# VectorE's order at joined pairs: the sum of the odd products, the next block's attention work and the masked copies change places in its queue

## The chip, the cores and the metric

The kernel runs on one core of one Trainium2 chip. A core has five engines that work side by side, each through its own queue of instructions in a fixed order: TensorE multiplies matrices (PE in the profile, and PEld for its weight loads), VectorE (DVE) works elementwise, ScalarE (ACT) computes functions and copies, GpSimd (POOL) and SyncE (SP) do little here but small fills and the issue of DMAs. Engines meet only at semaphores: an instruction whose input is not ready waits, and all that stands behind it in the same queue waits with it. TensorE writes its results to PSUM, a small memory from which VectorE and ScalarE fetch them. The metric is the device time of one execution in microseconds (us), lower is better. A profiled execution also leaves a trace, with the start and the duration of each instruction.

## The reference

Two parts, all in fp32. The first is a linear attention with a decaying state, for 4 batches, 8 heads, 768 tokens and a head size of 48; the second is a two-layer network over the 3072 tokens of width 384, with an inner width of 2048:

```python
for t in range(S):
    kt, vt, rt, wt = (k[:, :, t], v[:, :, t], r[:, :, t], w[:, :, t])
    cur = np.einsum('bhd,bhe->bhde', u[None] * kt, vt)
    y[:, :, t] = np.einsum('bhd,bhde->bhe', rt, state + cur)
    state = wt[:, :, :, None] * state + np.einsum('bhd,bhe->bhde', kt, vt)
...
x = np.ascontiguousarray(attn_out.transpose(0, 2, 1, 3)).reshape(B * S, H * D)
h = x @ w_in
g = h - np.tanh(h)
return (g @ w_out).astype(np.float32)
```

## The kernel before

**Blocks and tiles.** The tokens are cut into 8 blocks of 384 (half a batch each). The main loop (L1348) goes over the blocks `i`; within a block the loop over `f` (L1358) goes over the 16 tiles of 128 columns of the inner width. While the network of block `i` runs, the attention of block `i + 1` (`later`) is computed in pieces that stand between the tiles' work, and its first steps are taken one block earlier still (`after`). Which piece comes at which `f` is written in `plan` (L1142): `before` and `ahead` list VectorE's pieces, `phases` TensorE's and ScalarE's, `loads` the DMAs that are issued.

**One tile.** `first` (L893) multiplies the block by the tile's weights into the PSUM tile `hp`. `slight` (L974) has ScalarE compute two hyperbolic tangents of it and one square with a maximum check (L984, L985, L988), and leaves VectorE one product, `g` (L902), which is put into the list `rest` and runs in the next `f`.

**Second layer.** Two tiles make a pair `q = f // 2`. Instead of 18 products of 128 by 128 a pair takes 15, of sums of pieces of `g`: `form_g` (L1003, recorded at L1007) makes two such sums in one VectorE instruction. After an even tile there is one form (n = 0), after an odd tile one (n = 2), which the list `formed` holds; three more (n = 4, 6, 8) are held back to the next pair's time in `forming` and `carried`. `Fewer.add` (L1090) issues 12 of the 15 products into the PSUM tiles `acc`, in two halves, two and three steps after the odd tile (the list `due`, `add_due`). The remaining three, the odd products, go through `Fewer.others` (L1102) into a PSUM buffer `apart`: pairs 0 to 3 at `f` = 9, pairs 4 to 6 and pair 7 at `f` = 0 and 1 of the next block. `others_summed` (L1114, one VectorE instruction at L1115) then adds both halves out of `apart`.

**Joined pairs.** For some pairs both tiles' first layer is computed together with 11 products instead of 12: `Twos.begin` (L945, TensorE at L958, 22 recorded matmuls of 128 by 192). It writes both of the two PSUM buffers named `att`, and VectorE makes the two tiles of `h` of them by four sums `outs` (L968), with a copy by ScalarE (L959). `JOINED` (L123) says which: pairs 1, 3, 4 and 7 in blocks 3 to 6, so `f` = 2 and 3, 6 and 7, 8 and 9, 14 and 15; pairs 4 and 7 in block 2; pairs 0 to 6 in block 7, which has no `later`. The even `f` of a joined pair issues the products and the four sums, the odd `f` the tangents of the second tile.

**Who else uses the two `att` buffers.** The odd products (`apart`), the scores of the attention (`earlier`, L520, TensorE at L504) at `f` = 4 in blocks 3 to 6, which VectorE copies under a mask into the tile `scores` by two instructions (`masked`, L512), and the state update and the results (L585, L781) at `f` = 10 and 12.

**VectorE's queue.** It is written out by hand, at L1407 to L1444: for each `f` a list `ops` is put together out of

- `rest`: `g` of the tile before,
- `formed`, `forming`, `carried`: forms of `g`,
- `outs`: the four sums of a joined pair,
- `behind`: what a TensorE phase or `others` left for VectorE, the masked copies and `others_summed`,
- `spare`: pieces of attention work and, at some `f`, sums of the block before (`sum`, L1118, at L1123).

`between` interleaves two lists. The pieces of attention work that the change touches are `times_behind` (L449, at L453), `times_before` (L443, at L446; it finishes `pre`, which the scores at `f` = 4 read), `product_u` (L390, at L392; it reads the tile `k` that the DMA of L388 fills with tokens), `held` (L473), `product_r` (L394, at L396), `product_sum` (L398, at L400), and `before` (L423: a reciprocal and a scan at L427).

Of the kernel before, what the change touches and what calls it, by code (L numbers as in the profile page):

```python
# [122 lines left out]
JOINED = {2: (4, 7), 3: BESIDE, 4: BESIDE, 5: BESIDE, 6: BESIDE, 7: TWOS}  # L123
# [12 lines left out]
def kernel(  # L136
# [1005 lines left out]
    def plan(i):  # L1142


        formed_w = {}
        if i == 0:
            phases = {6: ("turn",), 7: ("update",), 10: ("earlier",), 13: ("results",)}
            before = {0: ("behind 2", "take_whole 2"), 2: ("behind 0", "take_whole 0"), 3: ("times_behind 2",),
                      4: ("times_behind 0",), 5: ("before 2",), 6: ("before 0",), 7: ("times_before",),
                      9: ("product_u", "held", "bound 2"), 10: ("product_r", "bound 0"), 11: ("product_sum",), 12: ("diagonal_in 2", "diagonal_in 0")}  # L1150
            ahead = {}
            loads = {f: "weights" for f in (0, 1, 3, 4, 5, 6, 7, 8, 9, 10)}
            loads.update({2: "next r", 11: "w", 13: "k", 14: "r"})
            loads = {f: [name] for f, name in loads.items()}
            loads[3] += ["v", "row"]
            loads[4] += ["tokens k"]
            loads[9] += ["tokens r"]
        else:
            phases = {3: ("split 2 0",), 4: ("earlier", "split 2 1", "turned 2", "split 0 01"), 5: ("turned 0",),
                      6: ("join 2 0",), 7: ("join 2 1",), 8: ("join 2 2",), 9: ("join 0 02",), 10: ("update",),  # L1160
                      12: ("results",)}
            before = {0: ("times_behind 2",), 1: ("times_behind 0",), 3: ("times_before", "held"),
                      5: ("product_u",), 6: ("product_r",), 7: ("product_sum",), 8: ("diagonal_in 2",),
                      9: ("diagonal_in 0",)}
            ahead = {10: ("bound 2", "bound 0"), 11: ("behind 2", "take_whole 2"), 12: ("behind 0", "take_whole 0"),
                     13: ("before 2",), 15: ("before 0",)}
            loads = {1: ["v"], 3: ["tokens k"], 4: ["tokens r"], 7: ["w"], 9: ["k"], 11: ["r"]}
            if i in JOINED:
                before = {0: ("times_behind 2",), 1: ("times_behind 0", "times_before 2"),
                          2: ("times_before 0",), 3: ("held",), 4: ("product_u",), 7: ("product_r",), 9: ("product_sum",),  # L1170
                          10: ("diagonal_in 2", "diagonal_in 0")}
                phases.update({3: (), 4: ("earlier", "turned 2")})
                loads = {2: ["tokens k"], 4: ["tokens r"], 5: ["v"], 7: ["w"], 9: ["k"], 11: ["r"]}
        if i == 1:
            phases = {4: ("split 2 0",), 5: ("split 2 1", "turned 2"), 6: ("split 0 01",),
                      7: ("earlier", "turned 0", "join 2 0"), 8: ("join 2 1",), 9: ("join 2 2", "join 0 01"),
                      10: ("join 0 2",), 11: ("update",), 13: ("results",)}
            before = {0: ("behind 2", "take_whole 2", "bound 2"), 1: ("behind 0", "take_whole 0"),
                      2: ("times_behind 2",), 3: ("before 2", "bound 0"), 4: ("times_behind 0",), 5: ("before 0",),
                      6: ("times_before", "held"), 7: ("product_u",),  # L1180
                      9: ("product_r", "product_sum", "diagonal_in 2"), 10: ("diagonal_in 0",)}
            ahead = {12: ("bound 2",), 13: ("behind 2", "take_whole 2"), 14: ("bound 0",)}
            loads = {1: ["v"], 4: ["tokens k"], 6: ["tokens r"], 9: ["w"], 11: ["k"], 12: ["r"]}
            formed_w = {2: (0, 1), 7: (2, 3, 4, 5), 9: (6,), 10: (7, 8), 11: (9,), 12: (0, 1), 13: (2, 3, 4, 5, 6),
                        14: (7, 8, 9)}
        elif i == 2:
            phases.update({3: (), 4: ("split 2 0",), 5: ("earlier", "split 2 1", "turned 2", "split 0 01"),
                           6: ("turned 0", "join 2 0")})
            before = {0: ("behind 0", "take_whole 0", "times_behind 2"), 1: ("times_behind 0",), 2: ("before 2",),
                      3: ("before 0",), 4: ("times_before", "held"), 5: ("product_u",), 7: ("product_r",),  # L1190
                      9: ("product_sum",), 10: ("diagonal_in 2", "diagonal_in 0")}
            loads = {1: ["v"], 3: ["tokens k"], 5: ["tokens r"], 8: ["w"], 10: ["k"], 11: ["r"]}
        return phases, before, ahead, loads, formed_w
# [17 lines left out]
    def converting(pieces, n):  # L1211

        made = []
        for _ in range(n):
            if not pieces:
                on_act, on_dve = convert(*raws.pop(0))
                pieces += zip(on_act, ([], [], on_dve))
            op, then = pieces.pop(0)
            op()
            made += then  # L1220
        return made
# [102 lines left out]
    def between(ops, others):  # L1324

        n = min(len(ops), len(others))
        return [op for pair in zip(ops, others) for op in pair] + ops[n:] + others[n:]
# [20 lines left out]
    for i, blk in enumerate(blocks):  # L1348
# [9 lines left out]
        for f in range(NF):  # L1358
# [9 lines left out]
            elif f % 2 == 0:  # L1368
                for op in behind:
                    op()  # L1370
                behind = []
# [3 lines left out]
                        later.phase(ps_a, name)  # L1375
            if not i:
                made_up = converting(pieces, PIECES[f] if f < len(PIECES) else 0)
            if joined and f == 9:
                fewer.others(ps_a, range(4), hp)
            if joined and f % 2:  # L1380
# [25 lines left out]
            if not now:  # L1406
                ops = square + converting(pieces, 2)  # L1407
            elif now == 1:
                ops = rest + late + square + converting(pieces, 3)
            elif not i:  # L1410
                ops = extra + square + (rest + behind + spare if f < 7 else rest[:1] + behind + spare + rest[1:])
            elif outs and near:
                ops = between(rest, carried) + spare + outs[:1] + formed + outs[1:]
                carried = []
            elif outs and later:
                ops = between(rest, carried) + outs[:1] + formed + outs[1:] + spare
                carried = []
            elif outs:
                ops = (between(rest, carried) + outs[:1] + formed + spare[:-1] + outs[1:2] + spare[-1:] + outs[2:])
                carried = []  # L1420
            elif joined and later:
                ops, carried = forming[:1] + rest + formed + spare, forming[1:]
            elif joined and f < 2 * LAST:
                ops, carried = forming[:1] + between(rest + formed, spare), forming[1:]
            elif joined:
                ops = forming[:1] + between(rest, forming[1:])
            elif carried:
                ops, carried = between(rest + formed, carried + behind + spare), []
            elif forming:
                ops = between(rest, forming[:2]) + square + formed + forming[2:]  # L1430
                ops = (between(ops, behind) if len(behind) > 2 else ops + behind) + spare
            elif adding and f % 2:
                ops = adding[:2] + between(rest, adding[2:3]) + square
                adding = adding[3:]
            elif adding:
                at = n_whole + n_excess
                ops = (between(rest, behind) +
                       [lambda: nc.vector.tensor_single_scalar(holds[:, n_whole:at], excess, 0.0, op=ALU.is_le),
                        lambda: sum_held(holds[:, at:at + n_top - 2], top[:, 0:n_top - 2], holds[:, 0:at + n_top - 2],
                                         ends[:, 0:1])] + adding[:4] + square + adding[4:])  # L1440
            elif square:
                ops = (between(rest, behind) if len(behind) > 2 else rest + behind) + square + formed + extra + spare
            else:
                ops = between(rest + formed, behind + spare)  # L1444
# [50 lines left out]
            for name in loads.get(f, ()):  # L1495
# [8 lines left out]
                    ins = of.load_v() if name == "v" else of.load(name.split()[-1])  # L1504
                if ins:
                    begin_behind(made, ins)
            if f < 2 and summed:
                summed[0].others(ps_a, ((4, 5, 6), (7,))[f], None if later else hp)
                if f:
                    behind.append(summed[0].others_summed)  # L1510
            add_due(now)
# [94 lines left out]
```

## Time and profile before

| | us |
|---|---|
| median of 3 runs | 545.23 (544.53 to 546.56) |
| profiled execution, its own time | 545.7 |
| its span, first to last instruction | 543.9 |
| TensorE matmuls busy | 529.9 |
| TensorE weight loads busy | 438.2 |
| VectorE busy | 462.7 |
| ScalarE busy | 309.7 |

The profile of one execution is read in several views. The page gives busy time, the granted clock of TensorE and the chain of work that ended last, followed back from the last instruction. The view of the waits adds up who waited for whom: the total, the number of times and the longest. The timeline lists instructions in the order of time: start in us, duration in us, engine, line, operation, written tile `<-` read tiles, shape, and how many like ones in a row (`x8`); in brackets stands the idle time of the engine ahead of it and what ended it. A matmul in fp32 is recorded twice, so the 11 products of a joined pair are 22 records. Matmuls are pipelined: the next one starts before the one ahead has ended, and how far apart two of them start tells more than the end that the record gives.

### The profile page before, as it was taken

Reading aid. Unit: us, or ns where it says so; the run is one execution under the profiler, and the core shown is the slowest. Engines: PE = TensorE matmul, PEld = TensorE weight load, DVE = VectorE, ACT = ScalarE, POOL = GpSimd, SP = SyncE. Lnnn points to the kernel's source line nnn. Section 1 sums busy time; section 2 is a strip of 40 time slices with the busy share of each in tenths; the row PEclk is TensorE's granted clock in tenths of the full one; section 3 lists DMA queues with packets and bytes.
Section 4 is the critical chain, followed back from the end, with each engine's and each line's share of the span. In section 5 each row is a group of like instructions: output and inputs, shape, how many; then the busy total and the mean of one; then the engine's idle time right before and its main releaser. Section 6 shows DMA issues by size and latency. Waiting matters only on the chain.

```text
span 543.9 us, 14925 instructions
## 1 busy us (share of the span) xinstructions
PE 529.9 (97%) x5950; PEld 438.2 (81%) x5950; DVE 462.7 (85%) x970; ACT 309.7 (57%) x720; POOL 9.1 (2%) x57
## 2 busy tenths in 40 slices
PE   7999999999999999999999999999999999999996
PEld 5756665678787978989898888889888897899994
DVE  7889996799899798978997899977999779777874
ACT  5899984665536564547546374364735545435460
POOL 1100000000000000000000000000000000000001
PEclk9899999999999999999999999999999999999999
DMA  7798642343312532270313712146231510100011
GB/s 276 245 390 332 239 120 70 123 111 89 99 46 61 147 117 57 63 167 20 119 56 74 176 60 68 47 109 141 64 96 34 135 39 1 57 1 2 11 34 46
DMA packets 53046, 56.33 MB, mean 104 GB/s; under 512 B 21488, under 2 KB 50928, under 8 KB 52976
## 3 DMA queue, kind: packets, MB, share of 16 engines
q1 hardware_dynamic: 52592, 55.18, 34.2%
q8 instruction: 49, 0.80, 0.6%
q14 instruction: 21, 0.17, 0.1%
q10 hardware_dynamic: 288, 0.10, 0.1%
q0 software_dynamic: 96, 0.07, 0.1%
HBM read 44.73 MB, written 4.72 MB: 91 GB/s over the span
## 4 chain that ended last, share of the span: by engine, by line
PE 76%; DVE 19%; issue 2%; DMA 1%; ACT 1%; SPq 0%; DVEq 0%
PE hp L895 20%; PE acc L1088 20%; PE att L958 14%; PE acc L1039 6%; DVE g L1007 4%; PE hp L1088 3%; DVE pre L427 2%; PE att L504 2%; DVE post L439 2%; PE att L781 2%; DVE g L902 2%; PE att L1088 2%; PE att L585 2%; DVE states L597 1%; PE acc L1066 1%
## 5 line engine op out<-in xcount | busy, mean ns | idle before, releaser
L895 PE MATMUL hp<-xT,w_sb 128*128 128x384 f32 x438 | 154.2, 488 | 0.0
L1088 PE MATMUL acc<-forms,g 128*128 128x128 f32 x972 | 136.4, 276 | 0.0
L1088 PEld LDWEIGHTS acc<-forms,g 128*128 128x128 f32 x972 | 124.2, 192 | 4.6 <-DVE g L1007 0.3
L895 PEld LDWEIGHTS hp<-xT,w_sb 128*128 128x128 f32 x438 | 78.6, 190 | 44.1 <-issue 1.4
L1007 DVE TENSOR_TENSOR g<-g 128x256 f32<-128x256 f32 x270 | 107.4, 421 | 4.6 <-PE acc L1088 0.3
L902 DVE SCALAR_TENSOR_TENSOR g<-h,qa 128x384 f32<-128x384 f32 x112 | 61.9, 552 | 37.5 <-ACT h L988 37.0
L984 ACT ACTIVATE h<-hp 128x384 f32<-128x384 f32 x73 | 36.3, 497 | 94.0 <-PE hp L895 93.7
L988 ACT ACTIVATE h<-h 128x384 f32<-128x384 f32 x113 | 58.7, 519 | 0.0
L958 PE MATMUL att<-xT,w_sb 128*128 128x192 f32 x250 | 53.4, 328 | 2.3 <-DVE scores L512 2.3
L1088 PE MATMUL acc<-w_sb,g 128*128 128x128 f32 x324 | 54.7, 278 | 0.0
L1088 PEld LDWEIGHTS acc<-w_sb,g 128*128 128x128 f32 x324 | 46.3, 191 | 5.8
L968 DVE TENSOR_TENSOR joint<-joint,att 128x384 f32<-128x384 f32 (+1 forms) x72 | 34.6, 501 | 13.7 <-PE att L958 9.1
L984 ACT ACTIVATE h<-joint 128x384 f32<-128x384 f32 x36 | 18.6, 518 | 44.6 <-DVE joint L968 44.6
L958 PEld LDWEIGHTS att<-xT,w_sb 128*128 128x128 f32 x250 | 41.4, 190 | 3.1 <-DVE scores L512 3.1
L985 ACT ACTIVATE qa<-hp 128x384 f32<-128x384 f32 x73 | 36.1, 494 | 0.0
L1123 DVE TENSOR_TENSOR sums<-sums 128x256 f32<-128x256 f32 x84 | 33.0, 411 | 1.4 <-ACT sums L1100 0.9
L1039 PE MATMUL acc<-w_sb,sums 128*128 128x384 f32 x96 | 33.7, 487 | 0.0
L271 ACT ACTIVATE up<-raw 128x768 f16<-128x768 f32 (+1 forms) x32 | 33.0, 1110 | 0.0
L1039 PEld LDWEIGHTS acc<-w_sb,sums 128*128 128x128 f32 x96 | 18.1, 190 | 12.3
L958 PE MATMUL att<-turned,kept 128*128 128x192 f32 x126 | 25.0, 329 | 1.0 <-DVE sums L1115 1.0
L427 DVE TENSOR_TENSOR_SCAN pre<-w,start 128x780 f32<-128x780 f32 x14 | 25.0, 1783 | 0.8
L439 DVE TENSOR_TENSOR_SCAN post<-w,seed 128x780 f32<-128x780 f32 x14 | 24.9, 1776 | 0.8 <-DMA w<-in_wT 0.8
(157 smaller groups left out, 769.1 us busy)
## 6 DMA issues: line engine op xcount, KB each, us to landing
raw<-in_weights SPq DMA_DIRECT2D x16, 768.0 KB, 7.8
w<-in_wT SPq DMA_DIRECT2D x7, 780.0 KB, 5.9
k<-in_kT SPq DMA_DIRECT2D x7, 768.0 KB, 4.7
r<-in_rT SPq DMA_DIRECT2D x7, 768.0 KB, 4.4
v_sb<-in_v SPq DMA_DIRECT2D x8, 576.0 KB, 4.1
k<-in_tokens SPq DMA_DIRECT2D x7, 576.0 KB, 3.9
r<-in_tokens SPq DMA_DIRECT2D x7, 576.0 KB, 5.3
out_y<-sums SPq DMA_DIRECT2D x18, 128.0 KB, 1.9
```

The source lines that it names most:

```text
L427: return nc.vector.tensor_tensor_scan(out=self.tile("pre")[:, cols], data0=self.tile("w")[:, cols], data1=start[:, 0:n * NCH * LP], initia ...
L439: return nc.vector.tensor_tensor_scan(out=back(t[:, 0:width]), data0=back(self.tile("w")[:, a:a + width]), data1=back(seed[:, 0:width]), i ...
L895: nc.tensor.matmul(hp, lhsT=w_in_sb[:, f, kc, :], rhs=xT[kc], start=(kc == KC - 1), stop=(kc == 0))
L902: return lambda: nc.vector.scalar_tensor_tensor(out=out, in0=in0, scalar=scalar, in1=in1, op0=op0, op1=ALU.mult)
L958: nc.tensor.matmul(to, lhsT=lhs, rhs=rhs, start=n == 0, stop=n + 1 == len(of))
L968: return [lambda of=of: nc.vector.tensor_tensor(out=of[0], in0=of[1], in1=of[2], op=ALU.add) for of in ((h[:, 0:5:4], twice(h[:, 3]), both ...
L984: made = nc.scalar.activation(out=t, in_=h, func=AF.Tanh, scale=INNER / UPSCALE)
L985: nc.scalar.activation(out=by, in_=h, func=AF.Tanh, scale=OUTER / UPSCALE)
L988: nc.scalar.activation(out=t, in_=t, func=AF.Square, accum_out=top[:, n:n + 1])
L1007: return lambda: nc.vector.tensor_tensor(out=G[:, to:to + 2], in0=two(G, g_at(q, a0), g_at(q, a1)), in1=two(G, g_at(q, b0), g_at(q, b1)), ...
L1039: nc.tensor.matmul(acc, lhsT=g[:, j * P:(j + 1) * P], rhs=w_out_sb[:, f, :], start=(f == self.first), stop=(f == NF - 1))
L1088: nc.tensor.matmul(to, lhsT=G[:, g_at(q, a), :], rhs=rhs, start=start, stop=stop, skip_group_check=True)
```

## The change

Only the order in which VectorE gets its work is edited, in blocks that have joined pairs and a `later`; no operation is added or left out.

- In the plan of blocks 3 to 6 the second half of `times_before` goes from `f` = 2 to `f` = 3, and `product_u` from `f` = 4 to `f` = 3, ahead of `held`.
- `others` of the block before is issued ahead of the tile's VectorE list instead of behind it (on TensorE its place is the same: behind `first`, ahead of `add_due`), and `others_summed` stands in `behind` at `f` = 1 and no longer at `f` = 2. At `f` = 1 it then comes behind the forms and ahead of `times_behind 0` and `times_before 2`. Block 7, without a `later`, keeps the old place.
- At the odd `f` of a joined pair `spare` goes from the end of the list to the second place, ahead of `rest` (`g` of the pair's first tile) and `formed`.
- At `f` = 5 of a block with joined pairs `behind` (the two masked copies in blocks 3 to 6) goes from the end of the list to its front.

```diff
             if i in JOINED:
                 before = {0: ("times_behind 2",), 1: ("times_behind 0", "times_before 2"),
-                          2: ("times_before 0",), 3: ("held",), 4: ("product_u",), 7: ("product_r",), 9: ("product_sum",),
+                          3: ("times_before 0", "product_u", "held"), 7: ("product_r",), 9: ("product_sum",),
                           10: ("diagonal_in 2", "diagonal_in 0")}
@@ -1375,6 +1375,10 @@
             if not i:
                 made_up = converting(pieces, PIECES[f] if f < len(PIECES) else 0)
+            if f < 2 and summed and later:
+                summed[0].others(ps_a, ((4, 5, 6), (7,))[f])
+                if f:
+                    behind.insert(0, summed[0].others_summed)
             if joined and f == 9:
@@ -1419,7 +1423,7 @@
             elif joined and later:
-                ops, carried = forming[:1] + rest + formed + spare, forming[1:]
+                ops, carried = forming[:1] + spare + rest + formed, forming[1:]
@@ -1428,7 +1432,8 @@
             elif forming:
                 ops = between(rest, forming[:2]) + square + formed + forming[2:]
-                ops = (between(ops, behind) if len(behind) > 2 else ops + behind) + spare
+                ops = (between(ops, behind) if len(behind) > 2 else
+                       behind + ops if f == 5 and i in JOINED else ops + behind) + spare
@@ -1504,8 +1509,8 @@
-            if f < 2 and summed:
-                summed[0].others(ps_a, ((4, 5, 6), (7,))[f], None if later else hp)
+            if f < 2 and summed and not later:
+                summed[0].others(ps_a, ((4, 5, 6), (7,))[f], hp)
                 if f:
                     behind.append(summed[0].others_summed)
```

## The prediction

> **What bounds the kernel now.** I read the page first: busy time, the granted clock, the chain that ended last.
>
> ```profile
> span 543.9 us, 14925 instructions
> ...
> PE 529.9 (97%) x5950; PEld 438.2 (81%) x5950; DVE 462.7 (85%) x970; ACT 309.7 (57%) x720; POOL 9.1 (2%) x57
> ...
> PEclk9899999999999999999999999999999999999999
> ...
> PE 76%; DVE 19%; issue 2%; DMA 1%; ACT 1%; SPq 0%; DVEq 0%
> ```
>
> TensorE is busy for 97% of the span at full clock, so what a new order on VectorE can win is what TensorE loses in waits for VectorE. Still 19% of the chain lies on VectorE: in stretches of each block it is VectorE that runs without a pause and TensorE that just touches it. The view of the waits, for TensorE and its weight loads, names the touching points (total, times, longest).
>
> ```profile
> PE att L958 <- DVE scores L512: 2.3, 4, 0.6
> ...
> PE att L781 <- issue: 1.7, 2, 1.1
> ```
>
> ```profile
> PEld att L958 <- DVE scores L512: 3.1, 4, 0.8
> PEld att L958 <- DVE sums L1115: 2.2, 4, 0.6
> ...
> PEld acc L1088 <- DVE g L1007: 0.3, 2, 0.2
> ```
>
> Three places wait for VectorE: joined products for the masked copies (f = 6) and for the odd sum (f = 2), four times each, which is blocks 3 to 6; and second-layer products for forms, twice. The timeline of one such passage (f = 0 to 6 of block 4) gives the price, if one goes by starts.
>
> ```profile
> 283.49 1.32 PE L1088 MATMUL acc<-forms,g 128*128 128x128 f32 x8
> 284.77 0.49 PE L1088 MATMUL acc<-w_sb,g 128*128 128x128 f32 x2
> 290.24 0.49 PE L958 MATMUL att<-turned,kept 128*128 128x192 f32 x2
> 291.05 0.92 PE L958 MATMUL att<-turned,kept 128*128 128x192 f32 x4 [0.32 <-DVE sums L1115]
> 303.13 0.61 PE L1088 MATMUL acc<-w_sb,g 128*128 128x128 f32 x4
> 303.58 1.06 PE L1088 MATMUL acc<-forms,g 128*128 128x128 f32 x8
> 305.22 1.24 PE L958 MATMUL att<-xT,w_sb 128*128 128x192 f32 x6 [0.59 <-DVE scores L512]
> 306.30 1.14 PE L958 MATMUL att<-turned,kept 128*128 128x192 f32 x6
> 307.27 0.49 PE L958 MATMUL att<-xT,w_sb 128*128 128x192 f32 x2
> ```
>
> Undisturbed, a 128x128 product starts 0.112 after the one ahead (303.13 to 303.58 over 4) and a 128x192 one 0.162 (306.30 to 307.27 over 6). So **masked copies**: after 303.58 + 8 x 0.112 = 304.48 the next could start, it starts at 305.22, 0.74 late; and the six after it take 1.08 instead of 0.97, another 0.11: 0.85. **Odd sum**: 290.24 + 2 x 0.162 = 290.56 against 291.05, 0.49, with the same 0.1 behind it 0.58. **Forms**: 283.49 + 0.90 = 284.39 against 284.77, 0.38, with 0.1 behind it 0.48.
>
> **The change part by part.** No operation comes or goes, so each part is worth the wait that it lifts, less any that it makes. The VectorE rows of the same passage:
>
> ```profile
> 280.28 0.56 DVE L902 SCALAR_TENSOR_TENSOR g<-h,qa 128x384 f32<-128x384 f32 x1 [0.71 <-ACT h L988]
> 281.48 1.78 DVE L427 TENSOR_TENSOR_SCAN pre<-w,start 128x780 f32<-128x780 f32 x1
> 283.18 0.54 DVE L902 SCALAR_TENSOR_TENSOR g<-h,qa 128x384 f32<-128x384 f32 x1
> 288.71 0.95 DVE L453 TENSOR_TENSOR post<-k,post 128x768 f32<-128x768 f32 x1
> 289.72 0.39 SPq L388 DMA_DIRECT2D k<-in_tokens  x1
> 290.44 0.55 DVE L1115 SCALAR_TENSOR_TENSOR sums<-att,o 128x384 f32<-128x384 f32 x1
> 290.91 0.55 DVE L902 SCALAR_TENSOR_TENSOR g<-h,qa 128x384 f32<-128x384 f32 x1
> 291.38 0.95 DVE L446 TENSOR_TENSOR pre<-r,pre 128x768 f32<-128x768 f32 x1
> 297.41 0.56 DVE L902 SCALAR_TENSOR_TENSOR g<-h,qa 128x384 f32<-128x384 f32 x1 [2.03 <-ACT h L988]
> 298.20 1.63 PE L504 MATMUL att<-pre,post 48*64 48x64 f32 x96
> 298.74 0.56 DVE L902 SCALAR_TENSOR_TENSOR g<-h,qa 128x384 f32<-128x384 f32 x1 [0.22 <-ACT h L988]
> 300.89 1.35 DVE L392 TENSOR_TENSOR k<-k,u_row 128x1152 f32<-128x1152 f32 x1
> 302.16 0.55 DVE L902 SCALAR_TENSOR_TENSOR g<-h,qa 128x384 f32<-128x384 f32 x1
> 304.17 1.90 DVE L512 COPY_PREDICATED scores<-mask_all,att 128x768 f32<-128x768 uint8 x2
> ```
>
> *Attention work ahead of g at f = 15.* VectorE stands 0.71 us for the tangents of the pair's first tile, and the scan comes after. Put ahead, the scan fills the wait: g of tile 15 moves from 283.18 to about 282.4, and with it the three forms behind it. The third wait (0.38 late) goes. The g held up by the scan feeds products that come two tiles later; no wait replaces the old one.
>
> *The odd sum at f = 1.* Today it stands behind two pieces of 0.87 (288.71 and what follows it, starts to 290.44). Put ahead of them it runs at 288.71 or, with the gain at f = 15, near 288: 1.7 or more earlier where 0.49 is needed. The two pieces move back by its 0.47, so g of tile 1 keeps its 290.91. The load of L388 waits for the first of them, since it overwrites `k`: it goes out up to 0.5 later, less the 0.8 won at f = 15.
>
> *Half of `times_before` and `product_u` to f = 3.* They cost 0.87 and 1.27 from start to start (291.38 to the next row; 300.89 to 302.16), with `held` some 2.2. There VectorE stands idle for 2.03 today, so they lie beside ScalarE's work. The excess of 0.2 moves g at 297.41, not the next g at 298.74, which waits 0.22 for ScalarE on its own account. If that cover were gone, 0.2 per block would reach the forms. Behind them the scores (L504, 298.20) need `pre`, finished near 295.5 after the shift: 1.5 or more to spare. At f = 5 `product_u` no longer stands ahead.
>
> *Masked copies first at f = 5.* They take the place of `product_u` at 300.89; the scores were written by 299.83, so they find them there. Two of them end near 302.8 on today's scale, and TensorE wants the buffers at 304.48: that wait (0.74 late) goes with 1.7 to spare, and with 0.6 if TensorE alone came 1.1 nearer. g of tile 4 then starts near 302.7, half a us later than today; its first products come at f = 7, over 4 us on, so nothing waits.
>
> *The other odd f.* At f = 7 and 9 about 2 us of attention work and sums moves ahead of g:
>
> ```profile
> 311.55 0.56 DVE L902 SCALAR_TENSOR_TENSOR g<-h,qa 128x384 f32<-128x384 f32 x1 [0.71 <-ACT h L988]
> ...
> 313.29 1.35 DVE L396 TENSOR_TENSOR k<-k,r 128x1152 f32<-128x1152 f32 x1
> ...
> 319.13 0.56 DVE L902 SCALAR_TENSOR_TENSOR g<-h,qa 128x384 f32<-128x384 f32 x1 [0.71 <-ACT h L988]
> ...
> 331.28 0.36 DVE L597 TENSOR_TENSOR states<-states,whole 128x192 f32<-128x192 f32 x1
> ...
> 331.93 1.56 PE L781 MATMUL att<-pre,states 48*48 48x64 f32 x96
> ```
>
> Each time a wait of 0.71 for ScalarE is filled, so what follows comes up to 0.7 earlier on top of TensorE's gain. That matters: from 319.13 on VectorE has no wait of note until f = 15, and the results (L781) start 0.29 after the last state update (331.28 + 0.36 = 331.64). TensorE will be 0.48 + 0.58 + 0.85 = 1.9 earlier there, and VectorE must be too: released by TensorE at f = 6 it moves 1.9, and I count 0.6 of the two filled waits on top, since at f = 10 it meets ScalarE. In block 2, only f = 9, 15 and the odd sum change; no wait of TensorE on them stands in the list, so I cost that at nothing.
>
> **Sum.** Copies 4 x 0.85 = 3.4. Odd sum: the list has 2.2 in four waits, three near 0.61 and one near 0.35; in starts 3 x 0.58 and some 0.3, so 2.0. Forms 2 x 0.48 = 1.0. Together 6.4 us. The profiled execution took 545.7 (span 543.9 and 1.8 around it): 539.3. The median shown is 0.5 lower, which gives 538.8; I predict **539.1**.
>
> What the trace cannot price is the pair of waits at L781 put down to "issue" (1.7 in two, none in the other blocks). I keep them, and let them vanish or double in the range. The Trainium skill (Runtime: NRT & Kernel Launch, section Instruction fetch mechanics) says that crossing an instruction block is mostly hidden; if these two are such crossings, which no row tells, they are not hidden here. By that page the term would be 0, by the row it is 1.7 either way.
>
> **The rivals.**
>
> *VectorE's long stretch does not come forward.* If ScalarE, not VectorE's own place, sets f = 9 to 12, the state updates stay late. TensorE then waits 1.9 - 0.29 = 1.6 at the results of blocks whose results begin with the state, the second halves of a batch, two of the four: 3.2 given back, 542.5. For it speaks the unbroken stretch from 319.13; against it that its start hangs on the joined sums, which come with TensorE.
>
> *No effect: the buffers are the limit.* All the large waits are for the two `att` buffers. If a buffer were simply held until then, order could not free it: 545.2. Against it: the scores lay finished at 299.83 and VectorE reached them at 304.17. The Trainium skill (Perfetto Trace Analysis, section Optimization Strategy) says that a consistent bubble can mean too little PSUM for the next tile; by that rule the 5.4 us of the first two terms stay and only the forms' 1.0 goes, 544.2 on the median's scale. The rows speak for the queue's order instead.
>
> *Slower: `product_u` meets its load.* At f = 3 it stands ahead of g, one tile earlier than now, and all of VectorE stands behind it. The view of line L388 has its load:
>
> ```profile
> DMA to landing us min/median/max: 3.9/4.2/7.4
> ```
>
> Issued near 289.7, the load lands by 293.9 in the median, and `product_u` wants it near 295.4: 1.5 to spare. A landing at 7.4 would cost 297.1 - 295.4 = 1.7, over four blocks about 6 after the small cover, which eats the whole gain; beyond that the kernel is slower, and at 8.5 us by some 4: 549. The 7.4 belongs to the crowded start of the kernel; I give it little.
>
> **How the numbers follow.** Forecast 0.71, long stretch 0.12, no effect 0.09, slower 0.05, 0.03 for the unforeseen, mostly a smaller gain. The range for 8 in 10 goes from 537.3 (538.8 less most of the 1.7) to 542.5 (the first rival). Half a per cent, about what a measurement of this kernel can tell from no change, is 2.7 us, so faster means below 542.5: the forecast, half of the first rival and a little more, 0.79; the same 0.15; slower 0.06.
>
> **What would show it.** Right: the waits of L958 for L512 and L1115 are gone from the list; the 0.71 waits for L988 at odd joined f and the 2.03 are gone or small; busy TensorE is as long as before in a span some 6 us shorter. The step at f = 3 fails if L392 has idle time ahead of it that a DMA ended; the long stretch if L781 waits for L597; the copies if L512 waits for L504 at f = 5. The number is wrong if TensorE's waits of "issue" grow, or if forms (L1007) at f = 4 or 8 become what it waits for.

## The result, and the profile after

| | before, us | after, us |
|---|---|---|
| median | 545.44 (544.53 to 546.56, 4 runs) | 538.62 (538.02 to 539.61, 4 runs) |
| ratio to before, 95% interval | | 0.9876 (0.9851 to 0.9901) |
| profiled execution, its own time | 545.7 | 538.27 |
| its span | 543.9 | 536.4 |

The kernel is 6.8 us faster. One execution each of e4_plan (1099.3 us, the profiled one, which is why e14_plan_again profiles that kernel once more), of e6_nospare (909.3) and of the kernel before in the series of e3_oddsum (1128.24) was disturbed; the ratios below leave these out, and without them no median below would move by more than 0.12.

The page of the kernel after, with the span, the busy time, the granted clock and the chain that ended last, by engine:

```profile
span 536.4 us, 14922 instructions
...
PE 526.9 (98%) x5950; PEld 437.5 (82%) x5950; DVE 462.5 (86%) x970; ACT 310.3 (58%) x720; POOL 9.1 (2%) x57
...
PEclk9899999999999999999999999999999999999999
...
PE 96%; DMA 1%; issue 1%; ACT 0%; DVE 0%; SPq 0%; PEldq 0%; PEld 0%; DVEq 0%
```

The chain is the line to look at: VectorE had 19% of it and has none left, TensorE went from 76% to 96%. VectorE's busy time is what it was (462.7, now 462.5), so nothing was saved there; it is only no longer waited for. The waits of TensorE, all that the view lists (total, times, longest):

```profile
PE att L319 <- POOL ident masks.py:199: 2.1, 1, 2.1
PE att L504 <- issue: 1.5, 1, 1.5
PE hp L895 <- issue: 0.7, 1, 0.7
PE att L504 <- ACT k L464: 0.3, 1, 0.3
```

No wait for VectorE is among them. The first, second and fourth lie in the first 25 us, ahead of the main loop. The two waits of L781 for "issue" are gone, and one of L895 has come.

VectorE now waits for TensorE where it was the other way round. Its own view of the waits:

```profile
DVE g L902 <- ACT h L988: 21.4, 27, 2.0
DVE joint L968 <- PE att L958: 11.0, 12, 1.0
DVE joint L968 <- ACT joint L959: 6.3, 10, 1.0
DVE sums L1115 <- PE att L1088: 3.4, 5, 1.9
```

The wait of g for ScalarE was 37.0 in 43 before. The 16 waits from f = 15 of block 2 to f = 9 of block 6, at f = 3, 7, 9 and 15, are filled with attention work; four of 0.6 have come at f = 10, where g meets ScalarE, as the prediction said. The last line is new: the odd sum, which held TensorE up, is ready to run before TensorE has made its input.

How much a block became shorter can be read from one instruction in two blocks, here the first product of the joined pair at f = 2. (The rows come from short windows, which cut the groups; only the starts are used.) Before:

```profile
289.26 0.98 PE L958 MATMUL att<-xT,w_sb 128*128 128x192 f32 x5
...
354.08 0.65 PE L958 MATMUL att<-xT,w_sb 128*128 128x192 f32 x3
```

After:

```profile
287.42 0.82 PE L958 MATMUL att<-xT,w_sb 128*128 128x192 f32 x4
...
350.26 0.98 PE L958 MATMUL att<-xT,w_sb 128*128 128x192 f32 x5
```

64.82 us from block to block became 62.84: 1.98 less, where the three prices of the prediction add up to 0.48 + 0.58 + 0.85 = 1.91.

### The profile page after: what moved, and what is told of

The parts are those of the page before. It is cut to its first block, busy times and chain, and to the rows that moved or that the text cites. A ratio compares the mean times of both kernels' runs of the same rounds, so it can differ in the third digit from the quotient of the medians.

```text
span 536.4 us, 14922 instructions
## 1 busy us (share of the span) xinstructions
PE 526.9 (98%) x5950; PEld 437.5 (82%) x5950; DVE 462.5 (86%) x970; ACT 310.3 (58%) x720; POOL 9.1 (2%) x57
## 4 chain that ended last, share of the span: by engine, by line
PE 96%; DMA 1%; issue 1%; ACT 0%; DVE 0%; SPq 0%; PEldq 0%; PEld 0%; DVEq 0%
PE acc L1088 27%; PE hp L895 27%; PE att L958 17%; PE acc L1039 6%; PE att L781 4%; PE hp L1088 3%; PE att L1088 3%; PE att L504 3%; PE att L585 2%; PE acc L1066 1%; PE att L895 1%; DMA r<-in_rT 1%; PE acc L895 1%; PE att L527 1%; PE att L689 1%
## 5 line engine op out<-in xcount | busy, mean ns | idle before, releaser
L895 PE MATMUL hp<-xT,w_sb 128*128 128x384 f32 x438 | 154.3, 488 | 0.7 <-issue 0.7
L1088 PE MATMUL acc<-forms,g 128*128 128x128 f32 x972 | 135.9, 276 | 0.0
L1088 PEld LDWEIGHTS acc<-forms,g 128*128 128x128 f32 x972 | 124.0, 192 | 4.3
L895 PEld LDWEIGHTS hp<-xT,w_sb 128*128 128x128 f32 x438 | 78.6, 190 | 43.5 <-issue 0.9
L1088 PE MATMUL acc<-w_sb,g 128*128 128x128 f32 x324 | 54.1, 276 | 0.0
L958 PE MATMUL att<-xT,w_sb 128*128 128x192 f32 x250 | 53.0, 326 | 0.0
L1088 PEld LDWEIGHTS acc<-w_sb,g 128*128 128x128 f32 x324 | 46.4, 192 | 5.5
L958 PEld LDWEIGHTS att<-xT,w_sb 128*128 128x128 f32 x250 | 41.4, 190 | 0.0
L958 PE MATMUL att<-turned,kept 128*128 128x192 f32 x126 | 23.9, 326 | 0.0
```

The lines of the kernel that those rows point to most:

```text
L895: nc.tensor.matmul(hp, lhsT=w_in_sb[:, f, kc, :], rhs=xT[kc], start=(kc == KC - 1), stop=(kc == 0))
L958: nc.tensor.matmul(to, lhsT=lhs, rhs=rhs, start=n == 0, stop=n + 1 == len(of))
L1088: nc.tensor.matmul(to, lhsT=G[:, g_at(q, a), :], rhs=rhs, start=start, stop=stop, skip_group_check=True)
```

## The experiments

Four edits make the change: the **plan** (half of `times_before` and `product_u` at f = 3), the **odd sum** at f = 1, **attention work ahead** of g at odd joined f, the **copies first** at f = 5. The kernels below do one alone, leave one out, or move work against the order. Their times, with the kernel before in the same series:

| label | what | us | before | ratio, 95% interval |
|---|---|---|---|---|
| e1_copies | copies first alone | 541.72 | 545.72 | 0.9922 (0.9901 to 0.9943) |
| e2_spare | attention work ahead alone | 542.04 | 545.72 | 0.9931 (0.9906 to 0.9957) |
| e3_oddsum | odd sum alone | 542.91 | 546.16 | 0.9953 (0.9933 to 0.9974) |
| e4_plan | plan alone | 547.59 | 545.72 | 1.0036 (1.0022 to 1.0049) |
| e6_nospare | all but attention work ahead | 546.07 | 545.76 | 1.0003 (0.9987 to 1.0018) |
| e7_nocopies | all but copies first | 538.63 | 545.76 | 0.9872 (0.9850 to 0.9894) |
| e12_two | attention work ahead and copies first | 538.46 | 545.72 | 0.9861 (0.9839 to 0.9884) |
| e13_only15 | copies first, attention work ahead at f = 15 only | 540.41 | 546.16 | 0.9888 (0.9857 to 0.9919) |
| e9_before_twice | before, and a scan twice | 552.93 | 545.76 | 1.0137 (1.0112 to 1.0162) |
| e10_after_twice | after, and a scan twice | 540.65 | 545.76 | 0.9908 (0.9887 to 0.9929) |
| e11_lateload | after, tokens k loaded later | 560.19 | 546.16 | 1.0251 (1.0223 to 1.0279) |
| e14_plan_again | plan alone, for its trace | 547.29 | | one run |

The traces were reduced to one more table. For each two successive matmul records I took the difference of their starts, and added these up by the lines of the two: L1088 to L1088 (inside the second layer, where forms are waited for), L958 to L958 (inside a joined pair, where the odd sum is waited for, and the steps behind each wait) and L1088 to L958 (the step into a joined pair, where the copies are waited for). The work is the same in all, so what a number is above the smallest of its column is waiting, or a slower clock.

| kernel | L1088 to L1088 | L958 to L958 | L1088 to L958 |
|---|---|---|---|
| before | 174.46 | 87.85 | 5.79 |
| after | 173.09 | 85.38 | 2.79 |
| e1_copies | 174.40 | 87.43 | 2.79 |
| e2_spare | 173.08 | 85.78 | 5.77 |
| e3_oddsum | 174.05 | 85.78 | 5.78 |
| e14_plan_again | 178.72 | 87.43 | 2.80 |
| e6_nospare | 178.40 | 85.38 | 2.79 |
| e7_nocopies | 173.08 | 85.38 | 2.79 |
| e12_two | 173.09 | 85.38 | 2.79 |
| e13_only15 | 173.40 | 85.87 | 2.79 |
| e9_before_twice | 181.73 | 88.13 | 5.78 |
| e10_after_twice | 175.24 | 85.38 | 2.80 |
| e11_lateload | 191.28 | 85.38 | 2.80 |

From before to after the three columns fall by 1.37, 2.47 and 3.00, together 6.84. The rest of the profiled 7.5 us is the waits of "issue" in the main loop, 2.2 before and 1.0 after in starts, less 0.6 by which the main loop began later in this execution.

### One edit alone

**e1_copies.**

```diff
-                ops = (between(ops, behind) if len(behind) > 2 else ops + behind) + spare
+                ops = (between(ops, behind) if len(behind) > 2 else
+                       behind + ops if f == 5 and i in JOINED else ops + behind) + spare
```

> The kernel before with the masked copies alone put first at f = 5. Theory (each wait of TensorE for VectorE has its own price and its own cause): the copies end near 304.0 on the scale of the trace of before, product_u still stands ahead of them, and TensorE wants the buffers at 304.5; the wait of L958 for L512 goes, 4 x 0.85 = 3.4 us, the waits for L1115 and for the forms stay: 542.0 us. Rival (VectorE's own unbroken stretch sets the pace, and an order within f = 5 does not shorten it): the time won at f = 6 comes back as a longer wait for L1115 at f = 2 or at the results, 545 us.

Measured 541.72. The third column falls to its floor and the second by 0.42, four times the 0.1 that follows a wait; the first stays. The odd sum's wait is untouched:

```profile
PE att L958 <- DVE sums L1115: 0.9, 3, 0.3
```

So the copies' wait was worth 3.4, and the time won at f = 6 was not given back further on: VectorE's stretch from f = 9 to f = 1 came forward with TensorE. The rival falls.

**e2_spare.**

```diff
-                ops, carried = forming[:1] + rest + formed + spare, forming[1:]
+                ops, carried = forming[:1] + spare + rest + formed, forming[1:]
```

> The kernel before with the attention work alone put ahead of g at the odd f of joined pairs (the plan, the odd sum and the copies as before). Theory: filling the 0.71 us wait for ScalarE at f = 15 brings all that follows 0.8 earlier, which lifts the wait for forms (2 x 0.48) and the wait for the odd sum too (about 2.0), though that instruction keeps its place; the wait for the copies stays, 3.4: 542.4 us. Rival (each wait needs its own edit): the odd sum's wait stays, 544.4 us.

Measured 542.04. The view of its waits has the copies' as before, and the odd sum's no more:

```profile
PE att L958 <- DVE scores L512: 2.3, 4, 0.6
```

The first column is at its floor, the second falls by 2.07. The odd sum kept its place in the list, and yet its wait is lifted, by work moved at the odd f of joined pairs; that most of this comes from f = 15, where a wait for ScalarE is filled, is shown by e13_only15 below. Edits and waits do not go one to one.

**e3_oddsum.**

```diff
+            if f < 2 and summed and later:
+                summed[0].others(ps_a, ((4, 5, 6), (7,))[f])
+                if f:
+                    behind.insert(0, summed[0].others_summed)
...
-            if f < 2 and summed:
-                summed[0].others(ps_a, ((4, 5, 6), (7,))[f], None if later else hp)
+            if f < 2 and summed and not later:
+                summed[0].others(ps_a, ((4, 5, 6), (7,))[f], hp)
```

> The kernel before with the odd sum alone at f = 1. Theory: L1115 runs 1.7 earlier, its wait (2.0 in starts) goes, the wait for forms at f = 0 (1.0) and that for the copies (3.4) stay: 543.6 us. Rival (the copies wait longer by what is won at f = 2, since VectorE's place at f = 5 does not depend on TensorE): 545 us or above, with a longer wait for L512.

Measured 542.91. In the trace the second column falls by 2.07, the first by 0.41, the third stays: 2.5 where 2.0 was expected. The copies' wait did not grow (2.3 in four waits, as before), which the rival wanted. That some of the forms' wait goes too was not foreseen; nearly all of it goes at f = 0 of block 4, and why is not shown.

**e4_plan and e14_plan_again**, one kernel.

```diff
                 before = {0: ("times_behind 2",), 1: ("times_behind 0", "times_before 2"),
-                          2: ("times_before 0",), 3: ("held",), 4: ("product_u",), 7: ("product_r",), 9: ("product_sum",),
+                          3: ("times_before 0", "product_u", "held"), 7: ("product_r",), 9: ("product_sum",),
```

> The kernel before with the plan alone changed: the second half of times_before and product_u at f = 3, there behind g and the form and not ahead of them. Theory (this piece is only free where it fills the wait for ScalarE): L504 at f = 4 waits for pre by about 1.1 us, the forms behind g of tile 3 come about 1.9 late, TensorE loses some 1.8 per block and no longer meets the copies (0.85 less): about 4 x 0.95 slower, 549 us. Rival (it only takes product_u from ahead of the copies, and that is a gain): 542 us.

> The plan alone once more, for its trace. The time as measured, 547.6 us. Theory: waits of L504 for pre (L446) and of L1088 for forms (L1007) at f = 4, together some 5.5 us over four blocks, in the place of the waits for the copies (3.4), with the waits for the odd sum still there. Rival (the attention work at f = 3 delays the copies instead): the wait of L958 for L512 is longer than 2.3 us.

Measured 547.59, slower than before by 1.9. The waits of e14_plan_again:

```profile
PE acc L1088 <- DVE g L1007: 2.3, 4, 0.6
...
PE att L958 <- DVE sums L1115: 0.9, 3, 0.3
PE att L504 <- DVE pre L446: 0.9, 4, 0.2
```

The copies are waited for no more, as expected, and instead the scores for `pre` and the second layer for forms. In starts the forms cost 4.3 more (178.72 against 174.46), L504 about 0.45 in each of four blocks, and the copies 3.4 less: 2.6 by the trace, 1.9 by the medians, against the 3.3 expected. The size was off because I took L504 to be held up from its first product. Only its second half needs the moved piece.

### One edit left out

**e6_nospare** is the changed kernel with the one line of e2_spare as before.

> The changed kernel with the attention work back at the end of the list at odd joined f; the plan, the odd sum and the copies stay as changed. Theory: at f = 3 the 2.2 us of attention work now stand behind g and ahead of the next g, so L504 at f = 4 waits for pre and the forms come late (the plan alone cost 1.9 us), and the forms' wait at f = 0 comes back (1.0); copies and odd sum stay free: 545 us, between 543 and 547. Rival (that part of the change matters at f = 15 only): 539.6 us.

Measured 546.07, the whole gain lost. The timeline of f = 3 and 4 of block 4 shows the mechanism (VectorE and TensorE only):

```profile
295.95 0.56 DVE L902 SCALAR_TENSOR_TENSOR g<-h,qa 128x384 f32<-128x384 f32 x1 [2.03 <-ACT h L988]
...
296.89 0.95 DVE L446 TENSOR_TENSOR pre<-r,pre 128x768 f32<-128x768 f32 x1
...
297.76 1.35 DVE L392 TENSOR_TENSOR k<-k,u_row 128x1152 f32<-128x1152 f32 x1
...
297.89 0.93 PE L504 MATMUL att<-pre,post 48*64 48x64 f32 x48 [0.23 <-DVE pre L446]
...
299.57 1.09 DVE L1007 TENSOR_TENSOR g<-g 128x256 f32<-128x256 f32 x3
...
300.05 0.71 PE L1088 MATMUL acc<-forms,g 128*128 128x128 f32 x4 [0.58 <-DVE g L1007]
```

VectorE stands idle for 2.03, then does 2.2 us of attention work that could have run in that time, and TensorE waits twice for what comes behind it. In the kernel after the same two pieces run inside the wait:

```profile
292.52 0.42 DVE L1007 TENSOR_TENSOR g<-g 128x256 f32<-128x256 f32 x1
...
292.86 0.95 DVE L446 TENSOR_TENSOR pre<-r,pre 128x768 f32<-128x768 f32 x1
...
293.73 1.35 DVE L392 TENSOR_TENSOR k<-k,u_row 128x1152 f32<-128x1152 f32 x1
...
295.00 0.17 DVE L475 TENSOR_SCALAR holds<-whole 128x24 bf16<-128x24 f32 x1
295.08 0.55 DVE L902 SCALAR_TENSOR_TENSOR g<-h,qa 128x384 f32<-128x384 f32 x1
```

So the plan is harmful by itself and free under the other edit. The rival (f = 15 only) falls.

**e7_nocopies** is the changed kernel with the line of e1_copies as before.

> The changed kernel with the masked copies back at the end of f = 5. Theory: product_u no longer stands ahead of them, so they end 1.3 earlier than before against a TensorE that is 1.1 nearer: from 298.5 in the trace after, g and four forms take 1.8, the copies 1.85, end 302.1, and TensorE wants the buffers at 302.05: 0.1 to 0.3 a block, 539.4 us. Rival (the place at the front is what lifts that wait): all of its 3.4 comes back, 542 us.

Measured 538.63, nothing lost at all. In its trace the copies stand behind g and the forms, and TensorE starts the joined pair without a wait:

```profile
299.71 1.91 DVE L512 COPY_PREDICATED scores<-mask_all,att 128x768 f32<-128x768 uint8 x2
...
300.39 1.06 PE L1088 MATMUL acc<-forms,g 128*128 128x128 f32 x8
...
301.29 1.14 PE L958 MATMUL att<-xT,w_sb 128*128 128x192 f32 x6
```

TensorE begins at 301.29, before the second copy has ended (301.62). In the kernel before, too, TensorE went on at 305.22 while the copies ran from 304.17 to 306.07. That corrects my reading: each copy frees one `att` buffer, the joined products begin with the first and come to the second eight records later. I had taken both copies as the condition, so there was 0.9 us more room than I counted. Moving `product_u` away from f = 4 lifts this wait as well as moving the copies does; e14_plan_again has the third column at its floor too.

**e12_two** leaves out both the plan and the odd sum.

> The kernel before with two of the four edits: attention work ahead of g at odd joined f, and the masked copies first at f = 5; the plan and the place of the odd sum as before. Theory (the other two edits are redundant beside these: at f = 2 the odd sum is then 0.6 or more ahead of its need, at f = 5 the copies 0.4 ahead of theirs): as fast as the changed kernel, 538.6 us. Rival (all four are needed): 0.3 us a block or more stays, 540 us or above, with waits of L958 for L1115 or L512 in the trace.

Measured 538.46, with all three columns at the floor, equal to the change within its spread. Two short edits carry all that the three kinds of waits cost. The medians are closer than the traces: from its first product to its last, the main loop of e12_two took 508.05 and that of the kernel after 506.50. Of this 1.2 lies in the waits of "issue" (see the end of the next section). The medians do not show it, and the clock can hide it: the four executions of e12_two list a granted clock of 0.998 or 0.999, three of the four of the kernel after one of 0.994 to 0.996, and what that is worth is shown with the next run.

**e13_only15** cuts one of these two down further.

```diff
+            elif joined and later and f == 15:
+                ops, carried = forming[:1] + spare + rest + formed, forming[1:]
             elif joined and later:
                 ops, carried = forming[:1] + rest + formed + spare, forming[1:]
```

> The kernel before with the copies first at f = 5 and the attention work ahead of g at f = 15 only, not at f = 3, 7 and 9. Theory (one filled wait, at f = 15, lifts forms and odd sum, and TensorE's coming forward at f = 6 brings VectorE's stretch with it): as fast as all four edits, 538.6 us. Rival (the two filled waits at f = 7 and 9 are needed, or the results wait for the state updates): up to 1.6 in two blocks stays, 540 to 542 us, with waits of L781.

Measured 540.41, between the two. In the trace 0.31 and 0.49 of the three columns stay above the floor, and TensorE's weight loads still wait for the odd sum, twice and shortly:

```profile
PEld att L958 <- DVE sums L1115: 0.6, 2, 0.3
```

So the fills at f = 3, 7 and 9 are worth some 0.8 beside it. No wait of L781 for the state updates is in the list, so that part of the rival falls. The other 1.1 us of the difference to e12_two is not in these columns. In the profiled executions the main loop's first product starts at 25.22 here and at 23.51 there, 1.7 apart, in a part that no edit touches. The clock differs there. The same window in both traces, e13_only15 first (us, then busy time and count of each engine; the third number from the end is the granted share of TensorE's clock, ahead of the DMA's two columns):

```profile
22.10:25.40 3.30, 3.30 (x92) 3.15 (x90) 1.89 (x6) 0.53 (x3) 0.22 (x4) 0.50 0.97 359
```

```profile
22.10:25.40 3.30, 3.30 (x70) 2.22 (x67) 2.98 (x9) 2.68 (x5) 0.09 (x1) 1.00 0.96 330
```

Half the clock for 3.3 us can cost up to 1.65 us. All four executions of e13_only15 list a granted clock of 0.996, against 0.998 or 0.999 for e12_two, so most of the other 1.1 us is likely this clock and not the edit.

### Work added and a load delayed

**e9_before_twice and e10_after_twice** add the same VectorE work to both kernels.

```diff
                 phases.update({3: (), 4: ("earlier", "turned 2")})
+                ahead = {**ahead, 13: ("before 2", "before 2")}
```

> The kernel before with one scan and its reciprocal done twice at f = 13 of blocks 2 to 5 (same values written again): 1.96 us more VectorE work in each of four blocks, in the stretch from f = 9 to f = 1. Theory (before, VectorE set the pace there and TensorE touched it): every one of them is paid, 4 x 1.9 = 7.6, 553 us. Rival (VectorE, busy for 85%, has room and only the order at the touching points counts): under 2 us, 547 us.

> The changed kernel with the same scan and reciprocal done twice. Theory (the order has given VectorE a lead of 1.4 to 2 us over TensorE from f = 9 to f = 2): most of 1.96 is taken by the lead; only the forms at f = 0 come some 0.4 late, 0.5 a block, 540.6 us, between 539.6 and 541.5. Rival (VectorE still sets the pace there and only the touching points moved): 546 us.

Measured 552.93 and 540.65. The 7.8 us (4 x 1.96) of extra work cost 7.2 before and 2.0 after. The waits for forms of the first:

```profile
PE acc L1088 <- DVE g L1007: 5.6, 7, 1.0
```

and of the second:

```profile
PE acc L1088 <- DVE g L1007: 0.2, 1, 0.2
```

This tells the two pictures of the kernel before apart. VectorE was busy for 85% of the span, and still in its stretch from f = 9 to f = 1 each added microsecond was paid. The order has given it a lead there, and three quarters of the added work vanish in it.

**e11_lateload** is the changed kernel with one load held back.

```diff
-                g, _, square, later_ops = slight(twos.h[0], now, i, f)
+                g, joint_made, square, later_ops = slight(twos.h[0], now, i, f)
...
-                    begin_behind(made, ins)
+                    begin_behind(joint_made if f == 2 and i in range(3, 7) and name == "tokens k" else made, ins)
```

> The changed kernel with the load of tokens k (L388) in blocks 3 to 6 held until the first tangent of the joined tile at f = 2, some 6 us later. Theory (product_u stands ahead of g at f = 3 with all of VectorE behind it, and 0.5 us of slack): it waits for the load by about 4 us, the forms that TensorE wants at f = 4 come 3 late or more, four blocks: 550.6 us, slower than before. Rival (ScalarE's wait at f = 3 covers it): 540 us or less.

Measured 560.19, 2.5% slower than before. VectorE's view of the waits:

```profile
DVE k L392 <- DMA k<-in_tokens: 18.4, 4, 4.9
```

and TensorE's:

```profile
PE acc L1088 <- DVE g L1007: 14.4, 4, 3.9
```

4.6 us of waiting for the load in each block became 3.6 on TensorE, so the mechanism is that of the theory, and the cover of some 1 us is soon used up. But the kernel lost 21.6 against the change where 12 were expected, and 15.0 is what the starts lost in those four waits. The rest is the clock. One block in windows, read as above:

```profile
304.20:307.75 3.55, 0.17 (x2) 0.00 (x0) 3.11 (x7) 0.00 (x0) 0.00 (x0) 1.00 1.53 287
308.10:311.50 3.40, 3.40 (x12) 2.49 (x12) 3.40 (x8) 0.00 (x0) 0.00 (x0) 0.50 0.36 80
311.50:315.00 3.50, 3.50 (x24) 3.10 (x23) 1.86 (x5) 1.37 (x4) 0.00 (x0) 1.00 0.20 18
```

After 3.5 us of idleness the granted clock is 0.50 for 3.4 us and then 1.00 again; windows of the other three blocks show 0.50 as well. That is 3.4 x 0.5 = 1.7 us a block, 6.8 in four, and 15.0 + 6.8 is the 21.6 lost within 0.2. The Trainium skill (TensorE: Matmul & The Clock Gate, section HAM oscillation — how this bites in real kernels) says that idle gaps above some 3.4 us bring TensorE back to half speed; this trace agrees, with gaps of 3.4 to 3.9 us and a clock of 0.50 behind each of the four.

## Why the prediction was right

**The bound.** It rested on TensorE as the limit, with three waits for VectorE that return in each block. The lists of waits before and after, and the chain at 96% TensorE, show that. Rival "no effect: the buffers are the limit" fell with e1_copies: an order alone freed them.

**The terms.** Copies 3.4: the step into joined pairs lost 3.00 and what follows it 0.4, so 3.4. Odd sum 2.0: 2.07. Forms 1.0: 1.37; the term was mis-sized because I took the two waits that the list names, and smaller ones of 0.1 in other blocks are not named there. The sum of 6.4 became 6.84, and the measured median lies 0.5 below the 539.1 forecast. That the medians also differ by 6.8 is in part luck: the profiled execution came out 1.0 below the 539.3 worked out for it, 0.4 by these terms and 1.2 by the waits of "issue", less 0.6 by the later start of its main loop. One sign came out otherwise: busy TensorE was to be as long as before and is 3.0 us shorter (529.9 to 526.9). Part of each wait had counted as busy, as the six products behind the copies' wait show (1.24 where the next six took 1.14).

**The steps.** At f = 15 the filled wait did what the prediction said, and more than I gave it: it lifts the odd sum's wait without help (e2_spare), so the edit at f = 1 is redundant, as is the plan (e12_two). That the plan is free only where it fills the wait at f = 3 held (e6_nospare; L392 has no idle time ahead of it in the kernel after). The room for the copies was counted too small (e7_nocopies), which did not touch the sum. "I count 0.6 of the two filled waits on top", said of f = 7 and 9, was more than was needed: the results do not wait for the state updates with those two left as they were (e13_only15). That TensorE's coming forward brings VectorE's stretch with it, as e1_copies had shown, is enough.

**The rivals.** "VectorE's long stretch does not come forward" is refuted by e1_copies and by e9 and e10 together: the stretch was the limit, and it moved. "Slower: product_u meets its load" is real, and e11_lateload shows it beyond its point of decision. The price expected of that run was too low: it counted the wait and not the clock, which added some half of it. For the delays of 1.7 to 2.8 us that the prediction itself priced no run shows a loss of clock: waits of TensorE of 1.0 us (e9_before_twice) and 1.7 us (e1_copies, at L781) left it at 1.00.

**The waits of "issue".** 1.7 was kept in the range. In the kernel after they are 0.7, at another line; in e12_two, just as fast, they are 1.7 at L781 again. They do not move at random. In the order of TensorE's 5950 matmul records they stand at the same two places in all thirteen traces read here. The first (0.3 to 0.6 us, before the 2374th record) is missing only in the kernel after. The second (0.6 to 1.7) stands before the 5442nd record, at L781, in the seven kernels without the plan, and before the 5444th, at L895, in the six that have it. So they belong to places in TensorE's program and not to VectorE; what ends them is not shown, and that the plan shifts one was not foreseen. What the Trainium skill says of crossings between instruction blocks (Runtime: NRT & Kernel Launch, section Instruction fetch mechanics) could be neither confirmed nor refuted by them.

## What to carry to other kernels

In a queue with a fixed order, look for an instruction that waits for another engine and has work behind it whose inputs have long been ready: that work goes in front, up to the length of the wait, and it helps at the far end of the stretch rather than where it stands. Price a wait by the distance of starts, with the slower steps behind it, and ask by adding work (e9, e10) whether an engine below full occupancy is nevertheless the limit in one stage. When several edits are made at once, do each alone and leave each out: here two of four carried all that the waits cost, and one was a loss by itself.

## What the runs showed of the hardware

- A wait of TensorE costs more than its idle time: the products that follow start 0.1 us late in sum (six in 1.08 instead of 0.97), behind each of the waits for VectorE looked at.
- A wait of 3.4 to 3.9 us also costs the clock: a granted clock of 0.50 for 3.4 us behind each of the four in e11_lateload, about 1.7 us more in each block. Waits in the main loop of 0.6 us (before), 1.0 (e9_before_twice) and 1.7 (e1_copies) left it at 1.00.
- The part ahead of the main loop differs from one execution to the next by up to 2.2 us, in programs that are the same there: the first product of the main loop started between 23.06 (e9_before_twice) and 25.22 (e13_only15). The clock goes with it. In four of the thirteen traces (before, after, e13_only15, e11_lateload) it is 0.50 for some 3.4 us between 21 and 26 us, and they start at 24.32 to 25.22; in the nine others it stays at 1.00, and they start at 23.06 to 23.87. Why it falls in some executions only is not shown.
- The same can be seen without a trace. Of the 37 executions of the kernel before that stand behind the ratios of the experiments, the 20 that list a granted clock of 0.998 or more have a median of 545.1, the 17 others one of 546.3. Differences under 0.4% between two profiled executions should be read from the main loop's rows and not from the span, and two medians 1 us apart should be compared at the same granted clock.
